# A planner that counts on later landings of the folded input and on heavier copies in DRAM

## The chip, the cores and the metric

The kernel runs on one core of a Trainium2 chip. The metric is the device time of one execution in microseconds. A core has a matrix engine (TensorE, PE in the profile), a vector engine (VectorE, DVE), a scalar engine (ScalarE, ACT), a general engine (GpSimd, POOL) and a queue engine (SyncE, SP). Each works through its own list of instructions strictly in order, and an instruction that has to wait holds everything behind it on its engine. DMA transfers are issued here from SP's list and, for a few, from ACT's.

## The reference

For 8 batches of 3136 tokens by 256 features, the reference takes a real Fourier transform along the tokens, mixes the features with complex weights, shrinks the result towards zero, transforms back, and applies a two-part mixing layer to what comes out:

```python
X = np.fft.rfft(x, axis=1)
Yr = Xr @ w_r - Xi @ w_i + b_r
Yi = Xr @ w_i + Xi @ w_r + b_i
Yr = np.sign(Yr) * np.maximum(np.abs(Yr) - 0.01, 0.0)     # Yi likewise
y = np.fft.irfft(Yr + 1j * Yi, n=3136, axis=1)            # x of what follows
h = xt @ U @ V                                            # xt: x with tokens last
u = x + h.transpose(0, 2, 1)
out = u + np.maximum(u @ w_ch1, 0.0) @ w_ch2
```

## The kernel before

The 3136 tokens are taken as 49 by 64, and the transform is done in two stages of small matrix products. While the window layers (the last two lines above, tiles `psy`, `psx`, `psz` and `pso` on PE) of one batch run, the transforms of later batches are slipped in between: stage a of batch b+2 (`psa`), stage b, mixing and stage c of batch b+1 (`psb`, `psq`, `pst`, `psc`), and the inverse of batch b+1 (`psd`).

From batch 3 on, stage a is *folded* (FOLD = 3): a row of tokens and its mirror row are added and subtracted first, which halves the matrix work. Three functions make up one folded load and its use, seven times a batch (u = 0 to 6):

- `f_turn` (line 745) copies the mirrored rows of x in DRAM into a scratch tensor `xd`, in eight DMAs a batch, issued by ACT.
- `f_load` (line 750) issues three loads on SP: 240 KB of x into `xa` (named `xt` in the profile), as much of `xd` into `xr`, and 10 KB of x into the last rows of `xr`. `xt` and `xr` have two buffers each.
- `f_prep` (line 761) lets VectorE add the two in place (`xr<-xt,xr`, the first reader of all three loads) and then subtract (`xt<-xt,xr`). ACT and POOL split each result into a high and a low part (`xh`, `xl`), and `f_mm` multiplies them on PE (`psa<-xh,ffh` and so on).

The inverse of a batch loads `zt` and `dt` on SP (lines 1144 and 1164) and multiplies them on PE (`psd<-dt,zt`). In stage b and c a swap of halves between partitions goes through DMA too (`ys<-tb`).

None of this is issued as it is written. All operations are recorded, and a planner (`_Program`) sets the order on each engine. `cost` gives every operation a duration; a DMA has in `move` its element count over 64,000, in us, and in `lag` 2.2 us plus that until its readers may start. `gap` (line 294) is the distance that a reader has to keep. `backward` turns the distances into due times, and `forward` builds the order: whatever is ready and due first goes next. There a DMA may start 16 us before it is due at the earliest (`lead`), DMAs move one after the other at their `move`, and SP issues the next when at most 2 us of moving are ahead of it and the eighth last has landed. Twelve such passes are made, the best is kept, and the program is then emitted in the order of the planned starts. The planned times themselves have no part in the execution: only the order stays, and the waits that the data demands.

Of the kernel before, what the change touches and what calls it, by code (L numbers as in the profile page):

```python
# [42 lines left out]
NK, NS = 125, 120  # L43
NU = 7
TURNS = 8
FOLD = 3
X0 = (0, 80, 176)
X0_PACE = (0.98, 0.92, 0.98)
# [110 lines left out]
PASSES, LEAD, FILL = 12, 16.0, 200.0  # L159
SWITCH, STICK, MARGIN, EARLY = 0.083, 5.0, 1.0, 0.0  # L160
# [5 lines left out]


class _Op:
    __slots__ = "n eng name args kw out cost lag move port fill start preds succs unit at lead".split()


class _Program:
# [15 lines left out]
    def record(self, eng, name, args, kw):  # L188
        op = _Op()
        op.n, op.eng, op.name, op.args, op.kw = len(self.ops), eng, name, args, kw  # L190
        op.preds, op.succs, op.lead = {}, [], LEAD
        out = kw["out"] if "out" in kw else args[0]
        views = [v for v in list(args) + list(kw.values()) if isinstance(v, _View)]
        op.out = out
        self.cost(op, out, [v for v in views if v is not out])
        for v in views:
            self.access(op, v, v is out)
        if self.behind is not None and op.eng in self.only:
            op.preds[self.behind.n] = self.behind
        self.ops.append(op)  # L200
        return op
# [67 lines left out]
    def order(self):  # L269
        ops = self.ops  # L270

        units = []
        for op in ops:
            last = units[-1] if units else None
            if op.eng == "pe" and last and last[0].eng == "pe" and last[-1].n == op.n - 1:
                a, b = last[0].out.buf, op.out.buf
                if a is b or a.key[1][:3] == b.key[1][:3] == "pso" and a.space == b.space == "psum":
                    last.append(op)
                    op.unit = len(units) - 1
                    continue  # L280
            units.append([op])
            op.unit = len(units) - 1
        size = []
        for u in units:
            t = 0
            for op in u:
                op.at = t
                t += op.cost
            size.append(max(t, u[0].move) if u[0].eng == "sp" else t)
        for op in ops:  # L290
            for e in op.preds.values():
                e.succs.append(op)

        def gap(e, op):

            if e.eng == op.eng and e.name != "dma_start":
                return e.at + e.cost + CHAIN.get(e.eng, 0.0)
            return e.at + e.cost + e.lag + (MARGIN if op.eng == "pe" else 0.0)


        tags = {}
        for op in ops:
            for v in list(op.args) + list(op.kw.values()):
                if isinstance(v, _View) and v.buf.first is op and v.buf.space != "dram":
                    tags.setdefault(v.buf.key, []).append(v.buf)
                    v.buf.first = (op,)

        after = [{} for _ in units]
        for k, u in enumerate(units):
            for op in u:  # L310
                for s in op.succs:
                    if s.unit != k:
                        g = gap(op, s) - s.at
                        after[k][s.unit] = max(after[k].get(s.unit, g), g)

        ideal, t = [], 0
        for u, n in zip(units, size):
            ideal.append(t)
            if u[0].eng == "pe":
                t += n  # L320
        late = [0.0] * len(units)
        for k in reversed(range(len(units))):
            v = ideal[k] if units[k][0].eng == "pe" else ideal[k] + 30
            late[k] = min([v] + [late[j] - g for j, g in after[k].items()])
        best = None
        for _ in range(PASSES):
            end, starts, fill, reuse = self.forward(units, size, tags, gap, late)
            if best is None or end < best[0]:
                best = end, late
            late = self.backward(units, size, after, reuse, gap, starts, end)  # L330

        late = best[1]
        for seed, share, low, high in CHANGES:
            late = self.changed(late, seed, share, low, high)
        end, starts, fill, reuse = self.forward(units, size, tags, gap, late)
        for k, u in enumerate(units):
            u[0].fill = fill.get(k, 0)
            for op in u:
                op.start = starts[k] + op.at
        return end  # L340
# [207 lines left out]
def fft_mix_moe_kernel(  # L548
# [21 lines left out]
    act, dve, pool, pe, dma = [prog.engine(e) for e in ("act", "dve", "pool", "pe", "sp")]  # L570
# [83 lines left out]
    xd = [dram.tile([24, N2, D], F32, name=f"xd{k}") for k in range(2)]  # L654
# [90 lines left out]
    def f_turn(b, k):  # L745
        m = slice(N2 // TURNS * k, N2 // TURNS * (k + 1))
        v = x[b].rearrange("(n m) d -> n m d", m=N2)[48:24:-1, m]
        act.dma_start(xd[b % 2][:, m].rearrange("n m d -> m n d"), v.rearrange("n m d -> m n d"))

    def f_load(b, u):  # L750
        n0, g = (10 * u, 2) if u < NU - 1 else (N2 - 5, 1)
        v = x[b].rearrange("(n m) d -> n m d", m=N2)[:, n0 : n0 + 5 * g]
        xa = fp.tile([NK, 2, D], F32, tag="xt", name=f"xt_{b}_{u}")
        xr = qp.tile([NK, 2, D], F32, tag="zt", name=f"xr_{b}_{u}", bufs=2)
        for t, w in ((xa, v[1:25]), (xr, xd[b % 2][:, n0 : n0 + 5 * g])):
            o = t[0:NS, 0:g].rearrange("p g d -> p (g d)")
            dma.dma_start(o, w.rearrange("n (j g) d -> n j (g d)", j=5))
        dma.dma_start(xr[NS:NK, 0:g].rearrange("j g d -> j (g d)"), v[0].rearrange("(j g) d -> j (g d)", j=5))
        a_state[b, u, "f"] = (xa[:, 0:g], xr[:, 0:g], n0)

    def f_prep(b, v):
# [27 lines left out]
    def f_spread(b, lo, hi):  # L789
        p = (hi - lo - 1) / (2 * NU - 1)  # L790
        us = [(lo - 2.5, lambda: f_load(b, 0)), (lo - 0.5, lambda: (f_prep(b, 0), f_load(b, 1)))]
        for v in range(2 * NU):
            def then(v=v):
                if v + 1 < 2 * NU:
                    f_prep(b, v + 1)
                    u = (v + 1) // 2 + 1
                    if v % 2 and u < NU:
                        f_load(b, u)

            us += [(lo + p * v, lambda v=v: f_mm(b, v)), (lo + p * v + 1, then)]  # L800
        return us
# [6 lines left out]
    def a_spread(b, lo, hi, u0=0):  # L808
        if b >= FOLD:
            return f_spread(b, lo, hi)  # L810
        p = (hi - lo - 1) / (NI // 2 - u0)
        us = [(lo - 2.5, lambda: (a_load(b, u0), a_load(b, u0 + 1))), (lo - 0.5, lambda: a_prep(b, u0))]
        for u in range(u0, NI // 2):
            def split_next(u=u):
                if u + 1 < NI // 2:
                    a_prep(b, u + 1)
                if u + 2 < NI // 2:
                    a_load(b, u + 2)

            us += [(lo + p * (u - u0), lambda u=u: a_mm(b, u)), (lo + p * (u - u0) + 1, split_next)]  # L820
        return us
# [508 lines left out]
    for a in range(4):  # L1330
        v = (b_r, b_i)[a % 2]
# [607 lines left out]
    for w, prev, next_w in zip(turn_w, [None] + turn_w, turn_w[1:] + [None]):  # L1939
        b, j = divmod(w, NW)  # L1940
        if j == 0 and b < NB:
            assert not side
            side = [(6.5, lambda b=b: rest_unit(b))]
            if b + 1 < NB:
                start, mid, end = (1, 58, 84) if b else (18, 71, 86)

                side += bmc_spread(b + 1, start, mid - 6)
                if b + 2 < NB:
                    if shared(b + 1):
                        lo, hi = (21, 56) if b == 0 else (1, 39)  # L1950
                    else:
                        lo, hi = 45, 94
                    side += a_spread(b + 2, lo, hi, 0 if b else AHEAD_A)
                if FOLD <= b + 3 < NB:
                    side += [(54 + 5 * k, lambda b=b, k=k: f_turn(b + 3, k)) for k in range(TURNS)]
                if b + 3 == FOLD:
                    side += [(BS - 4, f_setup)]
                side += spread(d_units(b + 1), mid, end)
                side += [(end + 1.5, lambda b=b: p_unit(b + 1))]
            else:  # L1960
                side += [(40, rest_load)]
            side.sort(key=lambda z: z[0])
        for g in range(2):
            l1s = l1_chunks(w, g)
            new = l2_chunks(w, g)
            for k in range(4):
                for c in range(2):
                    n = WS * j + 8 * g + 2 * k + c
# [131 lines left out]
```

## Time and profile before

| | us |
|---|---|
| median of 3 runs (lowest, highest) | 1621.2 (1620.72, 1626.43) |
| the profiled execution | 1620.49 |
| its span, first to last instruction | 1618.7 |
| PE busy in it | 1582.8 (98%) |
| VectorE, ScalarE, GpSimd busy | 1182.6, 1049.1, 533.6 |
| mean granted clock of PE | 0.998 |

The profile is of one execution. A busy share is an average over the whole span; where PE stands idle, and for whom, is read from the stretch concerned. In the rows, PE is the matmul, PEld the loading of its weights; a number in brackets is how long the engine stood idle ahead of the instruction, and behind the arrow what ended that. Nearly all instructions are emitted by one helper, line 538, so they are told apart by their tiles.

### The profile page before, as it was taken

How to read it: one execution, taken by the hardware profiler on the slowest of the kernel's cores; microseconds unless marked ns; L12 is line 12 of the kernel's file. 1: busy time of each engine (PE TensorE's matmuls, PEld its weight loads, DVE VectorE, ACT ScalarE, POOL GpSimd, SP SyncE). 2: the span in 40 equal slices, each digit the busy share in tenths (PEclk: the TensorE clock that was granted, in tenths of full speed). 3: DMA queues.
4: the chain of work that ended last, by engine and by line, in shares of the span. 5: the costliest groups of instructions: out<-in, count | busy, mean ns of one | idle time of the engine just before them, and what ended most of it. 6: DMA issues, size and time to landing. Idle time of an engine off the chain costs nothing.

```text
span 1618.7 us, 31635 instructions
## 1 busy us (share of the span) xinstructions
PE 1582.8 (98%) x11034; PEld 1467.2 (91%) x11034; DVE 1182.6 (73%) x2181; ACT 1049.1 (65%) x2340; POOL 533.6 (33%) x490
## 2 busy tenths in 40 slices
PE   9999999999999999999999999999999999999998
PEld 7869999999888899999988989999988999999998
DVE  6689776677857678578856878767885677856776
ACT  4768875576665776567755778556765677655553
POOL 2213442133433443123433444213342334212221
PEclk9999999999999999999999999999999999999999
DMA  9775536237654545414674555622657234630143
GB/s 241 213 229 172 150 111 156 74 100 187 184 165 146 162 131 137 129 53 131 172 199 138 157 152 131 166 76 81 160 151 213 82 92 120 153 83 16 40 87 53
DMA packets 295141, 218.22 MB, mean 135 GB/s; under 512 B 169167, under 2 KB 251942, under 8 KB 294982
## 3 DMA queue, kind: packets, MB, share of 16 engines
q1 hardware_dynamic: 283700, 207.71, 47.6%
q10 hardware_dynamic: 11282, 8.49, 1.8%
q8 instruction: 88, 1.44, 0.4%
q14 instruction: 71, 0.58, 0.1%
HBM read 128.43 MB, written 84.09 MB: 131 GB/s over the span
## 4 chain that ended last, share of the span: by engine, by line
PE 77%; DMA 12%; DVE 3%; ACT 2%; SPq 2%; issue 2%; POOL 1%; ACTq 0%; DVEq 0%; POOLq 0%
PE pso L538 27%; PE psy L538 14%; PE psx L538 7%; PE psq L538 6%; PE psd L538 6%; PE psb L538 4%; PE psz L538 3%; PE psc L538 3%; PE pst L538 3%; DMA xt<-in_x_dram 3%; PE psa L538 3%; SPq L538 2%; DMA xd<-in_x_dram 2%; DMA ys<-tb 2%; PE psv L538 1%
## 5 line engine op out<-in xcount | busy, mean ns | idle before, releaser
L538 PE MATMUL pso<-rh,w2t 128*128 128x512 f32 (+1 forms) x1600 | 410.0, 378 | 0.0
L538 PEld LDWEIGHTS pso<-rh,w2t 128*128 128x128 f32 x1600 | 280.2, 190 | 26.4
L538 PE MATMUL pso<-rl,w2t 128*128 128x512 f32 (+1 forms) x800 | 237.8, 376 | 0.1
L538 POOL TENSOR_TENSOR yl<-ys,yh 128x512 fp32r<-128x512 f32 x98 | 127.1, 1297 | 211.4 <-ACT yh L538 92.9
L538 PEld LDWEIGHTS pso<-rl,w2t 128*128 128x128 f32 x800 | 151.5, 190 | 21.2 <-DVE rl L538 0.5
L538 ACT ACTIVATE rh<-s 128x512 fp32r<-128x512 f32 x196 | 122.5, 629 | 74.2 <-DVE s L538 73.3
L538 DVE SCALAR_TENSOR_TENSOR rl<-s,rh 128x512 fp32r<-128x512 f32 x196 | 153.5, 787 | 16.9 <-ACT rh L538 14.6
L538 POOL TENSOR_TENSOR tl<-ts,th 128x256 fp32r<-128x256 f32 x88 | 66.7, 758 | 181.0 <-ACT th L538 55.8
L538 POOL TENSOR_TENSOR ocl<-xq,och 128x256 fp32r<-128x256 f32 x47 | 36.2, 770 | 268.0 <-DVE tt L538 162.4
L538 PE MATMUL psq<-wmt,xsh 128*128 128x256 f32 (+1 forms) x704 | 122.6, 275 | 1.0 <-ACT th L538 1.0
L538 PE MATMUL psy<-odh,w1t 128*128 128x256 f32 x784 | 121.8, 278 | 0.7 <-DVE s L538 0.7
L538 PEld LDWEIGHTS psy<-odh,w1t 128*128 128x128 f32 x784 | 111.5, 192 | 6.9 <-DVE s L538 1.4
L538 PEld LDWEIGHTS psq<-wmt,xsh 128*128 128x128 f32 (+1 forms) x704 | 110.3, 191 | 4.1 <-ACT th L538 1.4
L538 PE MATMUL psd<-dt,zt 98*128 98x130 f32 x896 | 110.9, 277 | 2.6 <-DVE xq L538 1.9
L538 PEld LDWEIGHTS psd<-dt,zt 98*128 98x128 f32 x896 | 107.8, 192 | 5.0 <-DVE xq L538 2.4
L538 ACT ACTIVATE xq<-psd 128x196 f32<-128x196 f32 x256 | 70.3, 331 | 57.7 <-PE psd L538 49.9
L538 DVE TENSOR_TENSOR tb<-psq,bias 128x512 f32<-128x512 f32 x88 | 60.2, 684 | 57.8 <-DMA ys<-tb 35.1
L538 ACT ACTIVATE yh<-ys 128x512 fp32r<-128x512 f32 (+1 forms) x101 | 62.9, 623 | 60.1 <-DMA ys<-tb 49.2
L538 DVE TENSOR_TENSOR v<-v,psy 128x512 f32<-128x512 f32 x98 | 66.6, 680 | 48.2 <-ACT v L538 27.7
L538 POOL TENSOR_TENSOR xl<-xt,xh 120x512 fp32r<-120x512 f32 (+2 forms) x47 | 60.1, 1279 | 120.4 <-DVE pa L538 19.8
L538 DVE SCALAR_TENSOR_TENSOR rl<-psy,rh 128x512 fp32r<-128x512 f32 x98 | 67.0, 684 | 42.5 <-ACT rh L538 42.2
L538 PE MATMUL psq<-wmt,xsl 128*128 128x256 f32 (+1 forms) x352 | 96.8, 275 | 0.0
(234 smaller groups left out, 4255.2 us busy)
## 6 DMA issues: line engine op xcount, KB each, us to landing
zt<-zd SPq DMA_DIRECT2D x128, 196.0 KB
zd<-zs SPq DMA_DIRECT2D x96, 256.0 KB
out_dram<-os SPq DMA_DIRECT2D x188, 128.0 KB
t<-gd SPq DMA_DIRECT2D x84, 256.0 KB
fb<-in_fb_dram SPq DMA_DIRECT2D x96, 128.0 KB
vw<-vd SPq DMA_DIRECT2D x96, 128.0 KB
ys<-tb SPq DMA_DIRECT2D x175, 64.0 KB
dt<-in_fd_dram SPq DMA_DIRECT2D x112, 75.0 KB
```

Of the source, the lines that this page charges most:

```text
L538: ins = call(*[real(a) for a in op.args], **{k: real(a) for k, a in op.kw.items()}).ins
```

## The change

Each recorded operation gets one more field, `slack`, 0 unless set. The three loads of `f_load` set it to 6.0, and `gap` adds it to the distance between a DMA and a reader on another engine: the planner takes each of them to land 6 us later than before. Each copy of `f_turn` has its `move` doubled. No operation is added, taken away or altered.

```diff
+AHEAD_X = 6.0
@@ class _Op
-    __slots__ = "n eng name args kw out cost lag move port fill start preds succs unit at lead".split()
+    __slots__ = "n eng name args kw out cost lag move port fill start preds succs unit at lead slack".split()
@@ record
-        op.preds, op.succs, op.lead = {}, [], LEAD
+        op.preds, op.succs, op.lead, op.slack = {}, [], LEAD, 0.0
@@ gap
-            return e.at + e.cost + e.lag + (MARGIN if op.eng == "pe" else 0.0)
+            return e.at + e.cost + e.lag + e.slack + (MARGIN if op.eng == "pe" else 0.0)
@@ f_turn
-        act.dma_start(xd[b % 2][:, m].rearrange("n m d -> m n d"), v.rearrange("n m d -> m n d"))
+        act.dma_start(xd[b % 2][:, m].rearrange("n m d -> m n d"), v.rearrange("n m d -> m n d")).move *= 2
@@ f_load
-            dma.dma_start(o, w.rearrange("n (j g) d -> n j (g d)", j=5))
-        dma.dma_start(xr[NS:NK, 0:g].rearrange("j g d -> j (g d)"), v[0].rearrange("(j g) d -> j (g d)", j=5))
+            dma.dma_start(o, w.rearrange("n (j g) d -> n j (g d)", j=5)).slack = AHEAD_X
+        dma.dma_start(xr[NS:NK, 0:g].rearrange("j g d -> j (g d)"), v[0].rearrange("(j g) d -> j (g d)", j=5)).slack = AHEAD_X
```

Since the planner weighs everything against everything, the order changes in nearly all of the program, not only at these operations. Three places follow. Names carry the batch and step (`xt_5_2` is batch 5, u = 2; `s1_21_0` is window 21), and a last number that rises in the order in which the plan first uses a tile, over all engines, so that it tells what stands where between engines; it differs a little between the two programs. Line 538 of before is line 539 of after.

VectorE at the third folded add of batch 5 (`xr_5_2<-xt_5_2`), before; `v12`, `s1`, `s5` and `rl` are steps of window 21, `xq` the result of window 20, `tb` the mixing of batch 4:

```order
L538 SCALAR_TENSOR_TENSOR tb_4_11_10626<-tb_4_11_10626,rl_4_11_10665 128x512
L538 TENSOR_TENSOR xr_5_2_10573<-xt_5_2_10663,xr_5_2_10573 120x512
L538 TENSOR_TENSOR s1_21_0_10651<-psz_21_0_10709,s1_21_0_10651 128x512
L538 TENSOR_TENSOR v12_21_0_10705<-v12_21_0_10705,psy_21_0_10623 128x512
L538 SCALAR_TENSOR_TENSOR xt_5_2_10663<-xt_5_2_10663,xr_5_2_10573 120x512
L538 SCALAR_TENSOR_TENSOR rl_21_0_0_10757<-s1_21_0_10651,rh_21_0_0_10738 128x2x256
L538 SCALAR_TENSOR_TENSOR rl_21_0_0_10757<-v12_21_0_10705,rh_21_0_0_10738 128x2x256
L538 TENSOR_TENSOR xq_3_0_8508<-xq_3_0_8508,pso_20_0_10389 128x16x32
L538 TENSOR_TENSOR xq_3_0_8508<-xq_3_0_8508,pso_20_1_10391 128x16x32
L538 TENSOR_TENSOR s5_21_0_10658<-psy_21_0_10623,s5_21_0_10658 128x512
```

And after, from the same step of `tb` on:

```order
L539 SCALAR_TENSOR_TENSOR tb_4_11_10639<-tb_4_11_10639,rl_4_11_10695 128x512
L539 TENSOR_TENSOR s1_21_0_10550<-psz_21_0_10706,s1_21_0_10550 128x512
L539 STREAM_TRANSPOSE os_19_10736<-xq_3_0_8489 128x16x32 x2
L539 TENSOR_TENSOR s5_21_0_10623<-psy_21_0_10534,s5_21_0_10623 128x512
L539 SCALAR_TENSOR_TENSOR rl_21_0_0_10701<-s1_21_0_10550,rh_21_0_0_10689 128x2x256
L539 TENSOR_TENSOR xq_3_0_8489<-xq_3_0_8489,pso_20_0_10364 128x16x32
L539 TENSOR_TENSOR xq_3_0_8489<-xq_3_0_8489,pso_20_1_10367 128x16x32
L539 SCALAR_TENSOR_TENSOR rl_21_0_1_10783<-s5_21_0_10623,rh_21_0_1_10758 128x2x256
L539 TENSOR_TENSOR xr_5_2_10455<-xt_5_2_10642,xr_5_2_10455 120x512
```

The add stood ahead of `s1`, `v12` and what follows them. Now eight instructions of that list, `s1`, `v12`, two `rl`, two `xq`, `s5` and one `rl` of the next step, have gone ahead of it (`v12` and one `rl` stand just above this piece). The loads of `xt_5_2` have the numbers 10663 and 10642, both shortly ahead of `psz_21_0` (10709 and 10706): the load keeps its place.

SP at the x load of batch 7, u = 4 (`xt_7_4`), before; `dt_6` and `zt_6` are inputs of the inverse of batch 6, `gd` and `vw` a stored result and a window input:

```order
L538 DMA zt_6_9_16178<-zd0_478 98x512
L538 DMA vw_35_16125<-vd_805 64x512
L538 DMA xr_7_4_16192<-xd1_5009 120x1x512
L538 DMA xr_7_4_16192<-in_x_dram 5x512
L538 DMA gd1_1054<-gs_7_5_16196 24x5x512
L538 DMA xt_7_4_16217<-in_x_dram 120x1x512
L538 DMA zt_6_10_16224<-zd0_478 98x512
L538 DMA dt_6_4_16232<-in_fd_dram 98x2x98
```

And after:

```order
L539 DMA xr_7_4_16051<-xd1_5003 120x1x512
L539 DMA zt_6_0_16060<-zd0_478 98x512
L539 DMA zt_6_1_16068<-zd0_478 98x512
L539 DMA zt_6_2_16079<-zd0_478 98x512
L539 DMA zt_6_3_16088<-zd0_478 98x512
L539 DMA zt_6_4_16096<-zd0_478 98x512
L539 DMA zt_6_5_16109<-zd0_478 98x512
L539 DMA gd1_1046<-gs_7_4_16084 25x5x512
L539 DMA xt_7_4_16134<-in_x_dram 120x1x512
L539 DMA zt_6_6_16149<-zd0_478 98x512
L539 DMA dt_6_2_16158<-in_fd_dram 98x2x98
L539 DMA dt_6_2_16158<-dud_1362 98x2x64
```

Before, the load stands behind the tenth input of the inverse (`zt_6_9`), after, behind the sixth and ahead of the seventh; the load of the copy (`xr_7_4<-xd1`) stands ahead of all of them. On VectorE the add of `xt_7_4` comes next to the reader of `psz_34_0` (number 16245) before, and next to that of `psd_6_10` (16243) after, so that 28 numbers lay between load and add, and now 109.

PE at the first product of the inverse of batch 4 (`psd_4_0`), whose input `zt_4_0` is loaded under the number 10843, before:

```order
L538 MATMUL psz_21_1_10879<-obh_21_10542,w1t_935 128x256 x4
L538 MATMUL psz_21_1_10879<-obl_21_10555,w1t_935 128x256 x2
L538 MATMUL psa_5_4_10890<-xh_5_4_10823,ffh_5174 125x512
L538 MATMUL psa_5_4_10890<-xh_5_4_10823,ffl_5198 125x512
L538 MATMUL psa_5_4_10890<-xl_5_4_10847,ffh_5174 125x512
L538 MATMUL pso_21_0_10836<-rh_21_0_1_10813,w2t_1255 128x512
L538 MATMUL pso_21_1_10838<-rh_21_0_1_10813,w2t_1255 128x512
L538 MATMUL pso_21_0_10836<-rh_21_0_1_10813,w2t_1255 128x512
L538 MATMUL pso_21_1_10838<-rh_21_0_1_10813,w2t_1255 128x512
L538 MATMUL pso_21_0_10836<-rl_21_0_1_10830,w2t_1255 128x512
L538 MATMUL pso_21_1_10838<-rl_21_0_1_10830,w2t_1255 128x512
L538 MATMUL psd_4_0_10916<-dt_4_0_10410,zt_4_0_10843 128x130 x4
```

And after, where `zt_4_0` has the number 10923:

```order
L539 MATMUL psy_21_1_10773<-odh_21_10650,w1t_935 128x256 x4
L539 MATMUL psy_21_1_10773<-odl_21_10675,w1t_935 128x256 x2
L539 MATMUL psy_22_0_10925<-oah_22_10892,w1t_935 128x256 x4
L539 MATMUL psy_22_0_10925<-oal_22_10915,w1t_935 128x256 x2
L539 MATMUL psx_22_0_10936<-och_22_10858,w1t_935 128x256 x4
L539 MATMUL psx_22_0_10936<-ocl_22_10889,w1t_935 128x256 x2
L539 MATMUL psd_4_0_10996<-dt_4_0_10441,zt_4_0_10923 128x130 x4
```

Before, the 15 matmuls shown ahead of the product (9 of 512 columns, 6 of 256) and 16 more above them (10 of 512, 6 of 256) stand behind the load. After, it is the 18 that are shown, all of 256 columns.

## Rows read from the trace of the kernel before

**Rows 1.** The page: span, and busy time of the engines.
```profile
span 1618.7 us, 31635 instructions
...
PE 1582.8 (98%) x11034; PEld 1467.2 (91%) x11034; DVE 1182.6 (73%) x2181; ACT 1049.1 (65%) x2340; POOL 533.6 (33%) x490
```

**Rows 2.** By stretch: length, busy us (instructions) of five engines, clock, DMA share, GB/s.
```profile
380.00:580.00 200.00, 190.06 (x1303) 176.05 (x1302) 141.67 (x261) 131.68 (x302) 82.80 (x71) 0.99 0.60 168
780.00:1000.00 220.00, 210.54 (x1452) 195.97 (x1451) 160.35 (x290) 148.45 (x340) 89.59 (x80) 0.99 0.57 161
1180.00:1260.00 80.00, 75.18 (x510) 68.79 (x509) 53.48 (x98) 49.39 (x112) 29.97 (x26) 1.00 0.65 179
...
1260.00:1600.00 340.00, 340.00 (x2367) 320.10 (x2367) 245.52 (x441) 201.37 (x423) 90.82 (x83) 1.00 0.34 82
```

**Rows 3.** Tile `xr`: idle us and times before its instructions, by what ended it.
```profile
  DMA xt<-in_x_dram: 27.8, 11
...
  issue: 10.5, 7
...
  DMA xr<-xd: 6.9, 4
```

**Rows 4.** Timelines of VectorE and PE: start, length, instruction [idle before <-releaser].
```profile
813.27 0.69 DVE L538 TENSOR_TENSOR xr<-xt,xr 120x512 f32<-120x512 f32 x1 [4.14 <-DMA xt<-in_x_dram]
813.88 0.68 DVE L538 TENSOR_TENSOR s<-psz,s 128x512 f32<-128x512 f32 x1
...
814.62 0.71 PE L538 MATMUL psy<-obh,w1t 128*128 128x256 f32 x4 [1.71 <-DVE s L538]
...
957.79 0.69 DVE L538 TENSOR_TENSOR xr<-xt,xr 120x512 f32<-120x512 f32 x1 [1.63 <-DMA xr<-xd]
```

**Rows 5.** By stretch: ten pauses of PE behind a folded add (three shown), their sum.
```profile
463.40:466.00 2.60, 0.66 (x6) 0.47 (x5) 1.61 (x4) 0.56 (x2) 0.00 (x0) 1.00 0.57 173
...
515.00:518.00 3.00, 1.72 (x14) 1.58 (x13) 2.53 (x7) 0.63 (x3) 1.27 (x1) 1.00 0.80 219
...
957.00:959.50 2.50, 0.94 (x5) 0.54 (x4) 1.71 (x4) 1.32 (x5) 0.44 (x1) 1.00 0.90 274
...
sum 27.80, PE 10.44 PEld 7.08 DVE 22.62 ACT 6.78 POOL 6.67; mean PE 1.04 PEld 0.71 DVE 2.26 ACT 0.68 POOL 0.67
```

**Rows 6.** By stretch: sum of three pauses behind the swap.
```profile
sum 9.10, PE 5.06 PEld 4.16 DVE 4.86 ACT 3.53 POOL 1.83; mean PE 1.69 PEld 1.39 DVE 1.62 ACT 1.18 POOL 0.61
```

**Rows 7.** The chain that ended last: start, us, what.
```profile
168.80 1.34 PE psq L538 x12
...
222.38 2.59 PE pso L538 x12
...
807.77 5.48 DMA xt<-in_x_dram
...
848.45 7.71 DMA xd<-in_x_dram
```

**Rows 8.** Timelines of SP, PE and ACT: an inverse load, a pair of copies.
```profile
1215.44 1.64 SPq L538 DMA_DIRECT2D zt<-zd  x4
...
1220.44 2.06 PE L538 MATMUL psd<-dt,zt 98*128 98x130 f32 x16 [0.42 <-DMA zt<-zd]
...
835.93 0.56 ACT L538 ACTIVATE xq<-psd 128x196 f32<-128x196 f32 x2 [4.82 <-DMA xd<-in_x_dram]
...
837.40 0.71 PE L538 MATMUL psy<-odh,w1t 128*128 128x256 f32 x4 [0.73 <-DVE s L538]
```

**Rows 9.** Waits: who <- for whom, us in total, times, longest.
```profile
PE psd L538 <- DMA zt<-zd: 0.6, 2, 0.4
...
SPq L538 <- DMA xd<-in_x_dram: 20.8, 13, 4.9
```

**Rows 10.** By stretch, behind the pause at 850 us; the clock is third from the end.
```profile
854.00:856.00 2.00, 2.00 (x12) 2.00 (x10) 0.90 (x2) 0.60 (x1) 0.16 (x1) 0.50 0.55 180
856.00:858.00 2.00, 2.00 (x16) 1.97 (x15) 0.22 (x1) 1.22 (x4) 0.00 (x0) 0.80 0.24 61
```

## The prediction

> **What bounds the kernel now.** I read the page first. TensorE (PE) is busy 1582.8 us of a span of 1618.7 [rows 1]: only the 35.9 us in which PE stands can be won without removing matmuls, and the change removes none. The second view is PE's busy time by stretch [rows 2]. It is to be read as "length less busy". 140 to 380, 580 to 780, 1000 to 1180 and 1260 to 1600 us are full to the hundredth (the last of the four is shown). In the three stretches in which batches 3 and 4, 5 and 6, and 7 go through the folded transform PE is idle 9.9, 9.5 and 4.8 us, 24.2 in all; the other 11.7 of 35.9 are the start and the tail. Those are the stretches that the change speaks of.
>
> Third, what stands idle there. The view of the folded tile `xr` says that its instructions' engines stood 27.8 us in 11 places for a load of x and 6.9 us in 4 for the load of the reversed copy [rows 3]. Nearly all of it is VectorE's add in `f_prep`. The timeline shows one place whole [rows 4]: the add starts at 813.27 after 4.14 us of waiting, behind it on VectorE's queue stand the sums `s` and `v`, which wait for nothing but their turn, and PE's next group starts 1.71 us late at 814.62 "after DVE s". So PE never names the load; it pays at second hand. I found ten PE pauses that follow such an add. In ten short windows, one around each, PE is busy 10.44 of 27.80 us: 17.4 us lost [rows 5]. Three more pauses follow another DMA, the swap `ys<-tb`: 9.10 less 5.06, 4.0 us [rows 6]. The change does not touch those.
>
> **The change part by part.** No operation, byte or tile is added or removed. What changes is what the planner believes. An x load of 61,440 elements was taken to land 2.2 + 0.96 us after it is issued; its readers now count 6.0 more, 9.2 us. The chain shows 5.48 us for one [rows 7]: the old count was 2.3 us short, the new one has 3.7 to spare. A copy of 49,152 elements counted 0.77 us of moving and now 1.54, so 3.0 us to landing become 3.7, and the chain shows one of 7.71 [rows 7]. Copies stay undercounted, that one by 4.0 us.
>
> *The adds.* At the pause of 814.62 the new order puts eight more VectorE instructions ahead of the add while its load keeps its place (the first two pieces of order ahead of this text). Starts there follow each other by 0.61 us [rows 4], so the add comes some 4.9 us later in VectorE's work, against 4.14 us of waiting: that wait goes. At the last pause, after 1241 us, it is the load that moves: six loads of inverse inputs and a store now come right ahead of it, the whole inverse of batch 6 having slid back (the next two pieces). I counted the same way for all 35 loads: the matmuls recorded between the load's issue and its add, at 0.216 us for 512 columns and 0.112 for 256 (twelve take 2.59 and 1.34 us [rows 7]). Before, 21 of the 35 have under 5 us of matmuls to hide in, the least 1.5 and the middle one 4.4. After, none has: the least is 5.7, the middle 10.1. With a landing of 5.5 us all are covered while SyncE (SP) keeps up. The seven pauses behind an x load go in full. Three hang on the copy or on something unnamed: 1.94 us in the window at 463.40 and 1.28 in that at 515.00, where the add waited for "issue", that is, for nothing that the profile shows [rows 3, 5], and 1.56 in that at 957.00 [rows 5], where the load of the copy ended the add's wait [rows 4]; 4.8 us. As copies stay undercounted I let half remain. From the adds: 17.4 - 2.4 = 15.0 us won; bounds 0 (each wait turns up one instruction later, at `ys<-tb`, which is already at some of these places) and 24.2 (all of PE's idle time there).
>
> By the Trainium skill, page "DMA: Bandwidth & Descriptors", section "Why a DMA increments its semaphore by 16 and not by 1", a DMA runs on the largest number of engines up to 16 that divides the slowest dimension on both sides. A copy's slowest dimension is 8, so by that rule it has half of the engines, and doubling its bytes makes up for that alone, not for loads running beside it. No row here gives engines per transfer, but 7.71 us against 3.7 counted agrees that doubling is too little. By that rule the three pauses stay whole, and the sum below ends 2.4 us higher.
>
> *The buffers.* An add that comes later holds its two x buffers longer, which could push the whole fold back. The order says not: the last folded matmul of batches 4, 6 and 7 stands after at most 1.2 us more matmul work than before. I put 0 for it, at most 1.2 a stretch.
>
> *The inverse loads.* What the adds gain in distance, others lose. PE's first inverse matmul of batch 4 stood behind 5.4 us of matmuls after its load `zt`, now behind 2.0 (the last two pieces of order); that of batch 2 now behind 3.5. The nearest row is the inverse of batch 6: load issued at 1215.44, PE starts at 1220.44 after 0.42 us of waiting, 5.0 us [rows 8]. Against 5.0 us the new places are short by 3.0 and 1.5. Over the run PE waited 0.6 us in all for such loads [rows 9], because SP usually runs ahead of the plan. Bounds 0 and 4.5; I take 3.0 lost.
>
> *The copies on ScalarE.* ScalarE issues them, and where two follow each other the second can hold it: ahead of 835.93 such a pair held ScalarE 4.82 us, and PE then paused 0.73 [rows 8]. The new order has 8 such pairs for 5. Three more at 0.73 is 2.2 at most, 0 at least; I take 1.0.
>
> *The clock.* Behind the pause at 850 us the granted clock is 0.50 for 2 us and 0.80 for 2 more [rows 10]; 0.50 is 1.2 GHz of 2.4. That costs 1.0 + 0.4 us, in which PE counts as busy. If the pause goes, so does this: 1.4 won, 0 at least.
>
> *The rest.* The order also changes where nothing is to be won, the stretches that PE already fills [rows 2]; they can only lose. I take 1.0, between the pauses of 0.73 and 1.71 us that rows show [rows 4, 8]; bounds 0 and 4.
>
> Sum: 17.4 - 2.4 - 3.0 + 1.4 - 1.0 - 1.0 = 11.4 us won. The profiled execution took 1620.5 us, so 1609.1. The median of the runs is 1621.2, 0.7 above it: 1610 rounded.
>
> **The rivals.** *A: the wait moves.* At two of the ten places a swap `ys<-tb` stands close, so VectorE, let through the add, may stop there; of 17.4 us only a third is kept, and with the losses above (5.0) almost nothing: 1620. For it: three pauses already belong to the swap [rows 6], whose count is unchanged. Against: at most places what follows the add are sums that start 0.61 us apart with no wait of their own [rows 4].
>
> *B: SP is held in front of the inverse loads; slower.* SP takes its queue in order, and the load of the reversed copy stands at its head until the copy has landed: 20.8 us in 13 places, the longest 4.9 [rows 9]. If such a hold falls right ahead of the `zt` loads, which now have less matmul work behind them, PE pays the hold and the shortfall, 4.9 + 3.0 = 7.9 us, at each of the three starts of an inverse inside the folds (batches 2, 4 and 6): 24 us lost against 14.4 won in the terms above (17.4 - 2.4 + 1.4 - 2.0), so 1630. It makes the kernel slower by 0.5% only from 7.5 us a start. Against it: the copies stand further ahead of their loads in the new order in 25 of 35 cases, and PE's waits for `zt` are now 0.6 us in two places.
>
> *C: the belief does not bind.* Loads are held by buffers, not by due times, so they cannot come earlier and the add's wait just shows later: 1618 by a fifth of the gain. The 35 distances in the order speak against it.
>
> **How the numbers follow.** Forecast 0.64, centre 1610, own range 1601 to 1615; A 0.20; B 0.08; C 0.08. A measurement of this kernel can tell about 0.5%, 8.1 us, from no change, so faster means under 1613.1 and slower over 1629.3. Faster: the forecast nearly whole, and a little of A and C, 0.66. Slower: most of B, 0.07. The same: 0.27. The range goes from 1601 (15.0 + 1.4 won with only 0.7 lost leaves 1604.8 on the profiled execution; 3.8 more is what the unexplained 2.8 us of fold idle and some of the swaps' 4.0 could give) up to 1621, which takes in A and C and leaves out B.
>
> **What would show it.** Right: in the view of `xr`, idle time for x loads falls from 27.8 us to under 8; PE's idle time in the three fold stretches falls from 24.2 to some 10 to 13; the stretches between stay full; the clock has one dip fewer. New waits of PE for `zt` at the inverses of batches 2 and 4 of 1 to 3 us each show that term. Wrong: waits of `xr` gone and PE as idle as before, with `tb` waiting for `ys<-tb` in their place (A); PE waits for `zt` or `dt` over 7 us a start (B); waits of `xr` for x loads still above 20 us (C).

## The result and the profile after

Four runs of the changed kernel took 1599.3 us at the median (1597.46 to 1602.69), four of the kernel before beside them 1621.3. The ratio is 0.986, with a 95% interval of 0.9834 to 0.9886: 22 us faster, where the prediction said 11 and its range ended at 1601. Measured once more, later, the ratio was 0.9852 (0.9825 to 0.9878). The profiled execution took 1597.46 us.

The page of the changed kernel, span and engines, beside [rows 1]:

```profile
span 1595.7 us, 31622 instructions
...
PE 1573.2 (99%) x11032; PEld 1463.6 (92%) x11032; DVE 1192.6 (75%) x2181; ACT 1052.2 (66%) x2340; POOL 536.2 (34%) x490
```

The span is 23.0 us shorter. PE's idle time fell from 35.9 us to 22.5, which is 13.4 of it. The other 9.6 came out of PE's *busy* time, which the prediction had taken as fixed but for 1.4. A second profiled execution of the changed kernel, of the same length (1595.6 us), divides its gain otherwise: 16.2 of idle time and 6.9 of busy time.

By stretch, as in [rows 2], the three stretches with folded batches (length, busy us of PE, PEld, DVE, ACT, POOL, then clock):

```profile
380.00:580.00 200.00, 195.18 (x1360) 182.35 (x1359) 151.76 (x272) 139.70 (x315) 86.73 (x75) 1.00 0.59 169
780.00:1000.00 220.00, 216.04 (x1508) 202.37 (x1507) 167.55 (x306) 157.16 (x352) 95.78 (x84) 1.00 0.58 164
1180.00:1260.00 80.00, 78.36 (x530) 72.47 (x529) 54.49 (x93) 51.51 (x114) 28.54 (x24) 1.00 0.54 154
```

Length less busy is 4.8, 4.0 and 1.6 us: 10.4 for the 24.2 before. The clock is 1.00 in all three, where it was 0.99 in two.

The waits (who <- for whom, us in total, times, longest), beside [rows 3, 9]. The add (`xr<-xt,xr` on DVE) no longer waits for any load of x or of the copy; that row is gone. In the view of the tile `xr`, the one of [rows 3], 3.7 us in one place are left for a load of x, on POOL. These waits are left:

```profile
ACT yh L539 <- DMA ys<-tb: 29.2, 29, 2.0
...
DVE tb L539 <- DMA ys<-tb: 22.3, 19, 2.8
...
PE psd L539 <- DMA zt<-zd: 1.5, 2, 0.9
...
SPq L539 <- DMA xd<-in_x_dram: 5.9, 5, 2.9
```

The last row is SP standing in front of a load of the reversed rows until the copy has landed: 5.9 us for 20.8. The first two are waits for the swap, which the change does not touch, and they fell too. Before, they read:

```profile
ACT yh L538 <- DMA ys<-tb: 49.2, 36, 4.0
...
DVE tb L538 <- DMA ys<-tb: 35.1, 27, 5.0
```

The clock, beside [rows 10]. The kernel before has a second dip, which [rows 10] do not show. First before, then after, at the places of its two dips (the clock is third from the end):

```profile
542.00:544.00 2.00, 2.00 (x7) 1.64 (x8) 2.00 (x4) 1.39 (x3) 1.20 (x1) 0.70 0.54 173
544.00:546.00 2.00, 2.00 (x8) 1.73 (x7) 2.00 (x5) 2.00 (x7) 0.00 (x0) 0.50 0.02 4
```
```profile
544.00:546.00 2.00, 2.00 (x20) 2.00 (x19) 1.82 (x3) 1.39 (x4) 2.00 (x2) 1.00 0.34 73
854.00:856.00 2.00, 2.00 (x18) 1.95 (x17) 0.86 (x3) 1.73 (x4) 1.01 (x1) 1.00 0.58 173
```

At 0.50 PE ran 8 matmuls in 2 us (12 in [rows 10]; the shapes differ), at 1.00 it ran 18 to 20, and all count as 2.00 us busy. From the start to PE's last matmul, in windows of two us one after the other, the time lost to the clock (one minus the clock, times two us) sums to 3.4 us before and to 0.0 after.

One new pause is of a kind that the prediction priced at 0.73 us. Timelines of ACT and PE in the changed kernel (start, length, instruction, idle before and what ended it):

```profile
444.52 0.65 ACTq L539 DMA_DIRECT2D xd<-in_x_dram  x1
445.22 0.60 ACT L539 ACTIVATE v<-psx 128x512 f32<-128x512 f32 x1 [4.87 <-DMA xt<-in_x_dram]
```
```profile
446.59 0.71 PE L539 MATMUL psy<-odh,w1t 128*128 128x256 f32 x4 [2.25 <-DVE v L539]
```

`v` itself reads no transfer. The issue of a copy stands right in front of it on ACT and got through only at 444.52, when, by the profile, a load of x had landed; PE paid 2.25 us. The same place cost 2.6 in the second execution. The copy reads nothing of that load. It waits for a counter (semaphore): the trace has it wait for the one that the load of x, issued at 436.82, counted up until 444.50, and that the copy counts up itself. Eight such counters serve all the DMAs of the program, so a DMA can stand behind another with which it shares no data.

### The profile page after: what moved, and what is told of

It is laid out like the page before. It is cut to its first block, busy times and chain, and to the rows that moved or that the text cites. A ratio compares the mean times of both kernels' runs of the same rounds, so it can differ in the third digit from the quotient of the medians.

```text
span 1595.7 us, 31622 instructions
## 1 busy us (share of the span) xinstructions
PE 1573.2 (99%) x11032; PEld 1463.6 (92%) x11032; DVE 1192.6 (75%) x2181; ACT 1052.2 (66%) x2340; POOL 536.2 (34%) x490
## 4 chain that ended last, share of the span: by engine, by line
PE 86%; DMA 7%; ACT 2%; DVE 2%; SPq 2%; issue 1%; POOL 1%; ACTq 0%; DVEq 0%; POOLq 0%
PE pso L539 30%; PE psy L539 15%; PE psx L539 7%; PE psq L539 7%; PE psd L539 6%; PE psb L539 5%; PE psz L539 4%; PE pst L539 3%; PE psa L539 3%; PE psc L539 3%; SPq L539 2%; DMA ys<-tb 1%; PE psv L539 1%; DMA zt<-zd 1%; DMA xt<-in_x_dram 1%
## 5 line engine op out<-in xcount | busy, mean ns | idle before, releaser
L539 POOL TENSOR_TENSOR ocl<-xq,och 128x256 fp32r<-128x256 f32 x47 | 35.9, 764 | 232.5 <-DVE tt L539 85.1
L539 DVE SCALAR_TENSOR_TENSOR rl<-psy,rh 128x512 fp32r<-128x512 f32 x98 | 67.2, 685 | 48.1 <-ACT rh L539 47.3
L539 ACT ACTIVATE v<-psx 128x512 f32<-128x512 f32 x98 | 58.4, 596 | 59.1 <-PE psx L539 53.3
L539 POOL TENSOR_TENSOR odl<-tt,odh 128x512 fp32r<-128x512 f32 x48 | 62.8, 1309 | 93.1 <-ACT odh L539 75.9
L539 PE MATMUL psb<-fb,t 128*128 128x128 f32 (+1 forms) x700 | 93.0, 276 | 1.1 <-issue 1.1
```

Source lines behind the costliest of these rows:

```text
L539: ins = call(*[real(a) for a in op.args], **{k: real(a) for k, a in op.kw.items()}).ins
```

## The experiments

### Which half of the change

Theory 1: the folded adds are the whole gain. Theory 2: they are two thirds, and the doubled copies give the rest by no longer holding SP. Theory 3: any new order would have done it.

```
e1_loads_only:   the copies' ".move *= 2" taken out
e2_copies_only:  AHEAD_X = 0.0
e3_nudged:       the kernel before with CHANGES = ((1, 0.5, 0.0, 1e9),)
e4_slack_2:      AHEAD_X = 2.5
```

`CHANGES` shifts every due time by a random amount (standard deviation 0.5 us) before the last pass: another order, the same beliefs.

> The 6 us on the loads alone, the copies counted as before. In its order all 35 x loads have at least 7.0 us of matmuls between issue and add, so VectorE's waits for x loads (27.8 us before) should be under 4 us. Theory 1 (the adds are the whole gain, the doubled copies are idle): 1598 to 1602 us, SP's waits for copies may stay near 20 us without harm. Theory 2 (the adds carry two thirds, the doubled copies the rest, by no longer holding SP in front of the swaps): 1605 to 1609, SP still waits some 15 to 20 us for copies and VectorE's `tb` some 25 us for swaps. Theory 3 (a new order by itself is worth this much): anywhere from 1600 to 1625.

> The doubled copies alone, the loads counted as before (21 of 35 adds have under 5 us of matmuls behind their load, as before the change). Theory 1: 1619 to 1623, waits of the adds for x loads still 25 us or more. Theory 2: 1612 to 1616, SP's waits for copies down from 20.8 to about 6 us and `tb`'s waits for swaps from 27.8 to about 16, the adds' waits unchanged. Theory 3: anywhere from 1600 to 1625.

> The kernel before, with every due time of the chosen plan nudged at random (standard deviation 0.5 us) before the last pass: a new order without a new belief; 21 of 35 adds still have under 5 us of matmuls behind their load. Theories 1 and 2: 1618 to 1625, waits of the adds for x loads 20 to 35 us. Theory 3: it may land below 1610.

> The change with 2.5 us in place of 6.0, about what the old count was short of the 5.5 us that a load takes; 4 of 35 adds have under 5 us of matmuls behind their load. If only the shortfall matters: 1599 to 1603, as with 6.0. If each added us is worth the same: 1610 to 1614 (2.5/6 of the gain kept), with some 15 us of waits for x loads left.

| | median us | ratio to before (95%) | waits of `xr` for x loads | SP's hold by copies |
|---|---|---|---|---|
| e1 loads only | 1608.1 | 0.9887 (0.9854 to 0.9919) | 0 | 16.0 |
| e2 copies only | 1616.1 | 0.9940 (0.9920 to 0.9961) | 32.8 in 15 | 15.4 |
| e3 nudged | 1627.4 | 1.0005 (0.9981 to 1.0030) | 23.2 in 12 | 18.3 |
| e4 slack 2.5 | 1604.2 | 0.9867 (0.9835 to 0.9899) | 10.7 in 6 | 16.5 |

A new order by itself, in the one that was tried, does nothing: theory 3 falls. Each half of the change gains, so theory 1 falls. The loads alone came as theory 2 has it. The run of the copies alone still has its x waits, as these waits of it show, and yet is 0.6% faster:

```profile
DVE xr L539 <- DMA xt<-in_x_dram: 32.8, 15, 4.9
...
DVE xr L539 <- DMA xr<-xd: 1.7, 1, 1.7
...
SPq L539 <- DMA xd<-in_x_dram: 15.4, 12, 3.2
```

Its time is at the edge of theory 2, its signs are not: SP's hold was to fall to about 6 us and `tb`'s wait for swaps to about 16, and they stand at 15.4 and 30.2. Where its 0.6% come from is not shown.

The 2.5 us of e4 are about the shortfall of 2.3 that the prediction read from a landing of 5.48 us against 3.2 counted; the 6.0 cannot be told from it. But only with both halves whole does SP's hold come down to 5.9. Neither total counts one for one in time: e4 keeps 10.7 us of x waits and 16.5 of hold.

### The waits alone, in an unchanged order

Here the order before is kept, instruction for instruction on every engine, and a wait is taken out by giving the instruction other data when it is issued. x1: the folded adds use a resident tile, so nobody waits for loaded x. x2: the load of reversed rows reads x instead of the copy, so it waits for no copy. x3: both. None of the three computes the transform: the loaded x, or the reversed rows, are left out of it.

```
x1   add.alt   = (), dict(out=sr, in0=one, in1=one, op=ALU.add)      # one: resident; sr, sa: a new tile
     twice.alt = (), dict(out=sa, in0=one, scalar=2.0, in1=sr, ...)  # xh, xl then read sr, sa
x2   load.alt  = (o, v[25:49].rearrange("n (j g) d -> n j (g d)", j=5))  # for xd[...]
```

Theory W: the x waits are the whole gain. A: in the old order the swaps would take them over. P: my sum. S: the hold of SP by copies delays what SP issues behind it, swaps above all. C: only three pauses hang on the copy. O: the new order has a gain of its own.

> The kernel before, with its order of instructions unchanged on every engine. Left out is the use of the loaded x in the folded batches: the add and the sum behind it read a resident tile and write a tile of their own, which the high and low parts then read, so nothing on VectorE, ScalarE or GpSimd waits for a load of x or of the reversed copy; the loads themselves still run, but no longer wait for a reader. Theory W (the waits for these loads are the whole gain, and nothing was lost elsewhere): 17.4 us of PE's idle time, some 1.5 us more that pauses cost in PE's busy time, and both clock dips, 3.4 us: 22 us, so a ratio of 0.986 and PE idle in the three fold stretches of 7 to 10 us. Theory A (swaps ys<-tb stand close behind and take the waits over, so part of the gain is the new order's own): a ratio of 0.991 to 0.995, VectorE's wait for swaps (tb<-ys) above 40 us. Theory P (my sum: 15.0 to 17.4 for the adds and 1.4 for one dip): 0.988 to 0.990.

> The kernel before, order unchanged, with one edit when instructions are issued: the load of the reversed rows reads the same number of rows of x itself instead of the copy, so it waits for no copy (the rows are not the reversed ones). The copies still run. This takes away SP's hold for copies (20.8 us in 13 places) and nothing else. Theory S (the hold delays what stands behind it on SP, the other loads and the swaps): 6 to 12 us faster, ratio 0.993 to 0.996, VectorE's waits for x loads under 20 us and for swaps under 30. Theory C (only three pauses hang on the copy): 3 to 5 us, 0.997 to 0.998, waits for x loads still 25 us or more.

> The kernel before with its order unchanged, and two things left out of the folded batches: the use of the loaded x (the add and the sum behind it read a resident tile and write a tile of their own), and the copy as the source of the reversed rows (the load reads as many rows of x itself). So neither VectorE nor SP waits for these transfers; all DMAs still run. Theory S (a hold of SP by a copy makes the swaps behind it late, which the run without the x waits alone showed at 517 us, 4.1 us of PE): ratio 0.984 to 0.987, no PE pause over 1.5 us behind a swap in the fold stretches, idle time there 8 to 11 us. Theory O (the new order has a gain of its own): 0.989 to 0.991.

| | median us | ratio to before (95%) | span, PE idle, in the folds | clock lost |
|---|---|---|---|---|
| before, profiled | | | 1618.7, 35.9, 24.2 | 3.4 |
| x1 no x waits | 1605.7 | 0.9897 (0.9862 to 0.9931) | 1610.0, 27.3, 15.7 | 3.4 |
| x2 no copy hold | 1619.5 | 0.9969 (0.9953 to 0.9984) | 1614.3, 30.8, 20.0 | 3.4 |
| x3 neither | 1599.4 | 0.9840 (0.9813 to 0.9867) | 1597.8, 21.3, 9.3 | 0.0 |
| after, profiled | | 0.9860 (0.9834 to 0.9886) | 1595.7, 22.5, 10.4 | 0.0 |

By the ratios the first wait alone is worth 1.0%, the second 0.3%, and both together 1.6%; the intervals are too wide to tell that from a plain sum. In the profiles the spans fall by 8.7, 4.4 and 20.9 us, but these are single executions: the one profiled of x1 was the slowest of its four (1611.84, median 1605.7), so its 8.7 is likely too low.

With both waits gone the old order runs as fast as the new one, so O (0.989 to 0.991 for x3) falls. W falls as it was put: x1 alone does not get there, and leaves 15.7 us of idle time in the folds for the 7 to 10 forecast. A wanted 0.991 or more and over 40 us of `tb` waiting for swaps in x1, where it is 36.5. The ratio of x1 is the one that P gave, 0.988 to 0.990. S holds for the ratio of x3 (0.984 to 0.987), but not in all that it forecast. The hold taken away by itself, in x2, gains about what C said (0.997 to 0.998, waits for x loads of 25 us or more), not S (0.993 to 0.996, x loads under 20, swaps under 30):

```profile
DVE tb L538 <- DMA ys<-tb: 30.6, 24, 3.0
...
DVE xr L538 <- DMA xt<-in_x_dram: 28.8, 12, 4.7
```

What x1 lacks is seen at one place. In x1, SP's waits from 495 to 513 us, then DVE and PE:

```profile
SPq L540 <- DMA xd<-in_x_dram: 7.1, 1, 7.1
```
```profile
508.13 0.77 SPq L540 DMA_DIRECT2D xr<-xd  x1
...
512.33 1.98 SPq L540 DMA_DIRECT2D ys<-tb  x2
...
514.80 0.69 DVE L540 SCALAR_TENSOR_TENSOR scr<-bias,scr 125x512 bf16<-125x512 f32 x1
...
519.96 0.69 DVE L540 TENSOR_TENSOR tb<-psq,bias 128x512 f32<-128x512 f32 x1 [4.48 <-DMA ys<-tb]
```
```profile
521.64 0.78 PE L540 MATMUL psa<-xh,ffh 120*120 120x512 f32 x1 [3.93 <-DVE tb L540]
```

and the same place in x3:

```profile
500.53 1.58 SPq L540 DMA_DIRECT2D xr<-in_x_dram  x2
...
510.97 1.18 SPq L540 DMA_DIRECT2D ys<-tb  x2
...
514.29 0.69 DVE L540 SCALAR_TENSOR_TENSOR scr<-bias,scr 125x512 bf16<-125x512 f32 x1
514.89 0.68 DVE L540 TENSOR_TENSOR tb<-psq,bias 128x512 f32<-128x512 f32 x1
```

In x1 the load of the reversed rows held SP for 7.1 us. When it got through, at 508.13, five more issues stood between it and the swap, which went out at 512.33, and the DVE instruction behind it (`tb`) stood 4.48 us. In x3 the load goes out at 500.53, right behind the load of x, the swap at 510.97, and `tb` follows its predecessor after 0.60 us without a wait. The later issue is only 1.4 of the 5.1 us by which `tb` starts later in x1. The rest is that the swap also took longer: 7.6 us from its issue to `tb`, for at most 3.9 in x3. The loads that the hold had kept back move in the same time (the DMA share from 512 to 514 us is 0.86 in x1 and 0.52 in x3); that they slow the swap is not shown. In x1 the pause is also followed by a clock dip:

```profile
518.00:520.00 2.00, 0.00 (x0) 0.00 (x0) 0.04 (x1) 0.03 (x1) 0.00 (x0) 1.00 0.43 143
520.00:522.00 2.00, 0.36 (x1) 0.36 (x2) 2.00 (x5) 0.98 (x2) 0.88 (x1) 0.73 0.20 48
522.00:524.00 2.00, 2.00 (x8) 1.70 (x8) 2.00 (x6) 1.87 (x5) 0.98 (x2) 0.50 0.21 70
524.00:526.00 2.00, 2.00 (x10) 1.97 (x10) 1.81 (x2) 0.84 (x3) 1.26 (x2) 0.50 0.29 66
```

So at this place the two waits lie in series, on two queues: the add gets through, and what follows it waits for the swap. Before, with both waits, the add stood 2.95 us here, `tb` did not wait, and PE paused 1.28 us.

But a swap can be late without a copy. S also said that x3 would have no pause of PE over 1.5 us behind a swap in the folds, and it has one, some 15 us further on, where SP had waited for no copy since 505 us:

```profile
528.07 1.17 SPq L540 DMA_DIRECT2D ys<-tb  x2
...
534.80 0.69 DVE L540 TENSOR_TENSOR tb<-psq,bias 128x512 f32<-128x512 f32 x1 [5.03 <-DMA ys<-tb]
```
```profile
535.54 0.48 PE L540 MATMUL psa<-xh,ffh 120*120 120x512 f32 x1 [2.44 <-DVE tb L540]
```

Over the whole of x3 the swap waits stay near those of before, 47.3 us for `yh` and 30.6 for `tb`. So their fall to 29.2 and 22.3 in the changed kernel is not brought by the end of the hold alone; its cause is open.

Two reservations. In x1 and x3 the loads of x have no reader and so find their buffers free earlier, which also relieves SP. In x1 SP's hold by copies did not fall for that, it rose (26.3 us for 20.8). And their new tile holds 16-bit numbers: POOL's split from it is shorter (means of 1.18 and 1.22 us for 1.33 and 1.35), the add longer (0.90 for 0.75).

### Is the gain the order's luck?

e6 is the changed kernel with the same random shift as e3; e5 counts x loads 12 us late (`AHEAD_X = 12.0`). B names the account of 13 us of idle and 9 to 10 of busy time; L says that half of it was luck.

> The changed kernel with its due times shifted at random by 0.5 us, another order that holds the same beliefs. If the gain belongs to the beliefs (theory W), it stays: a ratio of 0.985 to 0.990. If the half of it that I had not forecast is luck of one order (theory L): 0.991 to 0.994, with new PE pauses in the fold stretches, 17 us of idle time there or more.

> The changed kernel as it is, beside the others of this call. Theory B (its gain is two parts: 13 us of PE's idle time, the same in each execution, and 9 to 10 us of PE's busy time, of which 3.4 us are two clock dips that any one execution may have or not): a ratio of 0.985 to 0.988; in the profile PE idle 21 to 24 us, busy time 1573 us plus 1.7 us for each half of a dip that it shows. Theory L (half of the gain is luck of one profiled order or execution): 0.990 to 0.993.

> The changed kernel with x loads counted 12 us late instead of 6. Waits for x loads are gone at 6 and nearly at 2.5, so nothing is left to win there. Theory B: within 2 us of the changed kernel as long as the buffers allow it. If adds that come later hold their two buffers until the fold is pushed back: 5 to 15 us slower than the changed kernel, with PE waiting for the fold's pieces or for stores gd<-gs.

The shifted order gave 0.9876 (0.9841 to 0.9910), the kernel once more 0.9852 (0.9825 to 0.9878), 12 us for 6 gave 0.9847 (0.9822 to 0.9873). L, with 0.991 or more and 17 us of idle time in the folds, falls: e6 has some 11. The gain goes with the beliefs, and from 6 to 12 us it is flat. But what a single profile shows does vary: e6 lost 6.8 us to the clock and had a span of 1606.8; the changed kernel's second execution, at the same span as the first, lost 1.7 and had 20 us idle.

### What is left

The rest of the idle time in the folds stands behind swaps and inverse loads. The same means was tried on these: `.slack = 2.0` on the loads `ys<-tb` (f1), on `zt` and the last part of `dt` (f4), on all (f3); then only from batch 3 on, numbered from 0 as in the code (`2.0 if b > 2 else 0.0`): all (f5), all with `AHEAD_X = 12.0` (f6), swaps alone (f7).

> The changed kernel with the same means used on the next wait: readers of a swap ys<-tb count 2.0 us more. Waits for swaps are what is left most often on VectorE (22.3 us) and ScalarE (29.2 us), and some 3 us of PE's pauses stand behind them. If these pauses can be planned away as the others were: 2 to 3 us faster than the changed kernel, ratio 0.984, VectorE's wait for swaps under 15 us. If later swaps push the work that follows into other waits: no faster than the changed kernel, 0.986 to 0.990.

> The changed kernel with three more beliefs: 2.0 us more for readers of a swap ys<-tb, of an inverse load zt, and of the last part of a load dt. The run with the swaps alone had swap waits of 8 and 2 us instead of 22 and 29, but PE waited 8.1 us for dt and zt in place of 2.2. If that is what ate the swaps' gain: PE's waits for zt and dt under 3 us, PE idle 18 us or less, 2 to 4 us faster than the changed kernel. If each new count only hands the wait on to whatever is left uncounted: within 2 us of it.

> The changed kernel with 2.0 us more for readers of zt and of the last part of dt alone, swaps as they were. The term of my sum for the inverse loads, 3.0 us lost, is then taken away where the order allows it: PE's waits for zt and dt (2.2 us in the changed kernel) at 0 to 1. If those waits lie on the path: 1 to 2 us faster than the changed kernel. If they are handed on: within 1 us of it.

> The changed kernel with 2.0 us more for readers of swaps, of inverse loads zt and of the last part of dt, but only from the third batch on, so the first 300 us keep their plan (12 rows of filler matmuls as in the changed kernel). If the pauses left in the fold stretches are late transfers that can be planned away: idle time there 8 us or less for 10, PE's waits for zt and dt under 2 us, 2 to 3 us faster than the changed kernel, ratio 0.983. If the waits are only handed on: 0.985 to 0.988.

> As the one before, with x loads counted 12 us late in place of 6, which alone was 0.9847. Same forecasts: 0.982 to 0.983 if the counts add up, 0.985 to 0.988 if they only hand waits on.

> The changed kernel with 2.0 us more for readers of swaps alone, from the third batch on. With the same count in all batches the swap waits fell to 8 and 2 us, the clock dipped once and PE waited 8.1 us for inverse loads: 0.987. If its loss was the order of the first 300 us: 0.983 to 0.985. If it was the inverse loads: 0.986 to 0.988, with PE's waits for zt and dt at 5 us or more.

| | ratio to before (95%) | `tb` and `yh` for swaps | PE for `zt`, `dt` | idle in the folds | clock lost |
|---|---|---|---|---|---|
| f1 | 0.9872 (0.9846 to 0.9899) | 7.9, 2.0 | 8.1 | 11.6 | 3.4 |
| f3 | 0.9892 (0.9867 to 0.9917) | 13.7, 5.0 | 4.1 | 7.8 | 0.0 |
| f4 | 0.9898 (0.9876 to 0.9919) | 29.4, 28.6 | 5.3 | 16.4 | 5.1 |
| f5 | 0.9854 (0.9823 to 0.9884) | 17.9, 11.5 | 7.4 | 10.4 | 5.1 |
| f6 | 0.9844 (0.9813 to 0.9874) | 14.3, 12.4 | 4.0 | 7.2 | 3.4 |
| f7 | 0.9840 (0.9812 to 0.9869) | 15.0, 13.1 | 8.5 | 12.7 | 6.8 |

None can be told from the changed kernel to the better; f3 and f4 are slower than it by their medians. In f4 the waits that were counted, those of PE for `zt` and `dt`, did not go: 5.3 us for 2.2 in the changed kernel, where 0 to 1 was expected. Waits for swaps can be planned away almost wholly, as f1 shows, and it buys nothing: PE then waits for inverse loads instead.

```profile
DVE tb L539 <- DMA ys<-tb: 7.9, 7, 3.2
...
PE psd L539 <- DMA dt<-dud: 5.8, 3, 3.6
...
PE psd L539 <- DMA zt<-zd: 2.3, 3, 1.2
...
ACT yh L539 <- DMA ys<-tb: 2.0, 2, 1.8
```

f3 is the instructive miss: 7.8 us idle in the folds, no clock dip, and still 7.8 us longer in span than the changed kernel. Groups of PE instructions in f3 (count, busy us, mean ns):

```profile
L537 PE MATMUL psa<-ident 128*128 128x128 f32 x60 | 9.4, 323 | 2.1 <-POOL ident masks.py:199 2.1
L537 PE MATMUL psv<-ident 128*128 128x128 f32 x26 | 3.3, 278 | 0.0
```

These are dummy matmuls, which the planner puts where its own plan has PE standing early in the program. All groups with `ident` make 116 matmuls in f3, 18.1 us, for 54 and 10.8 us in the changed kernel beside it (16 in each are no dummies); most of the new ones stand from 114 to 128 us. The counts had made the plan of the start later, and 7.3 us went there, as busy time. Kept off the first batches (f5), the loss is gone, and no gain remains.

## Why the prediction was wrong

Direction and place were right, and so was the mechanism of the adds; the size was not, because what the waits cost beside PE's idle time was left out. By its own steps, in the profiled executions:

**"From the adds: 15.0 us won", less 3.0, 1.0 and 1.0.** That makes 10.0 us of idle time; 13.4 were won, 13.8 of it in the folds and 0.4 given back outside. Fold idle of 10 to 13 was forecast as the sign, and 10.4 is there. The 35 distances counted from the order were the right view: no wait of the add for x is left.

**"As copies stay undercounted I let half remain", 2.4.** This failed. No wait of the add for the copy is left either (6.9 us before). In the new order a copy stands 6.6 us of PE's matmuls ahead of its load in the middle case, for 5.1 before, and with SP's hold down to 5.9 us the loads behind it come on time. The rule of the Trainium skill (page "DMA: Bandwidth & Descriptors", section "Why a DMA increments its semaphore by 16 and not by 1") by which the prediction let the three pauses stay whole did not decide: the traces show them gone with the count doubled. The half of the engines that it gives a copy, eight, would fit the trace: the counter of the copy issued at 444.52 rises once at 445.61 and eight more times from 447.72 to 448.45.

**"I take 3.0 lost" for the inverse loads.** Too high: 1.5 us in two places; the one named, batch 4, waited 0.9. SP was ahead of the plan there, as the trace before had it: the load was issued at 816.93, 4.0 us before PE came to it, for 2.0 counted.

**"Three more at 0.73" for the copies on ScalarE.** The price was too low, and the place another: a single copy, not the second of a pair, was held, and cost PE 2.25 us, at 446.59, for the 1.0 taken.

**"1.4 won" for the clock.** I had looked behind one long pause; there were two dips, and both went: 3.4.

**"Only the 35.9 us in which PE stands can be won".** This is the step that failed most. PE's busy time fell by 9.6 us. Of these 3.4 are the clock. Another 3.4 or so are pauses that never show as idle: a matmul of 256 columns has a record of 275 ns on average, though twelve of them take 1.34 us [rows 7], so the next one can start some 0.16 us late before PE counts as idle. Added up from the timeline between 140 and 1580 us, delays of 0.05 to 0.6 us between starts are 21.3 us before and 15.4 after; about 2.5 of the former belong to the dips. These are estimates from one execution each. Of the remaining 2.8 us, some 1.3 are the dummy matmuls near the start (7.7 us before, 6.4 after); the rest I cannot place. In the second execution of the changed kernel, which lost 1.7 us to the clock and has 7.7 us of dummies, busy time fell by 6.9.

**Rival B saw the right queue and only its danger.** "SP is held in front of the inverse loads": SP's hold by copies was read as a risk for what stands behind it after the change, and never as a cost that the kernel before was paying already. x2 and x3 show that it was: by the ratios it costs 0.3% with the x waits in place and 0.6%, some 9 us, without them (x1 against x3). A was half right: in x1 the wait does move to `tb` at one place, where PE paused 3.93 us. In the changed kernel the longest pause that is left behind `tb` in the folds is 0.96 us. That it is gone there because of the doubled copies is likely from x3, but the swap waits fell too, for a reason that is open.

**The bounds.** The range ended at 1601 because it let PE's busy time fall by 1.4 us at most. With 13.4 for the idle time, 3.4 for the clock and as much for hidden pauses the forecast itself would have been 1600.

## What to carry to other kernels

When a planner's belief is put right, look for every queue on which the late transfer also holds others. Here the adds' waits alone were worth 1.0% of the time, the queue's hold alone 0.3%, and only both gave the 1.6%; that they are worth more together than as a sum is not shown. Do not take the busy time of the bounding engine as fixed: a slower clock and pauses shorter than an instruction's record hide in it, so measure the distances between starts around a pause, not the idle time. And a count that is put right in one place moves the start of the plan too: look at the filler work there before a gain in the middle is believed.

## What the runs showed of the hardware

Summed as above, the profiles of these kernels lost 0.0, 1.7, 3.4, 5.1, 6.8 or 10.2 us to a granted clock of 0.50, 1.2 GHz of 2.4. The dips in the folds came behind pauses of PE: 3.4 us were lost behind the 3.93 us above, 1.7 behind one of 1.84 at 541.98 in the kernel before. The length of the pause does not tell: the pause of 2.25 us at 446.59 was followed by no dip in one execution of the changed kernel and, at 2.6 us, by one of 1.7 us in another.

The issue of a DMA can hold the engine that does it. Ahead of `v` ACT did nothing for 4.87 us, of which 0.65 are the issue of a copy at 444.52; until then it stood in front of that issue. By the trace the issue waited for a counter that a load of x counted up until 444.50, though the copy runs from DRAM to DRAM and does not read that load.
